# Splitting fifteen of eighty loads into two transfers of unequal partition counts

## The chip, the cores and the metric

The kernel runs on one core of a Trainium2 chip. The metric is the device time of one execution in microseconds, the median over runs. Inputs and outputs are float32; inside, the kernel works largely in bfloat16.

## The reference

A gated linear attention with a recurrent state is followed by a gated MLP that mixes over the sequence. Batch 4, 8 heads, 768 steps, head size 48; the MLP has a width of 384 and 1024 hidden columns.

```python
def _attn_ref(q, k, v, alpha):                    # each (4, 8, 768, 48)
    for t in range(S):
        state = alpha[:, :, t, :, None] * state + einsum('bhd,bhe->bhde', k[:, :, t], v[:, :, t])
        y[:, :, t] = einsum('bhd,bhde->bhe', q[:, :, t], state)

def _moe_ref(x, w_in, w_spatial, b_spatial, w_out):   # x = y as (4, 768, 384)
    h = maximum(x @ w_in, 0)
    u, v = h[..., :512], h[..., 512:]
    v_n = (v - mean(v)) / sqrt(var(v) + 1e-6)
    v_s = einsum('ts,bsd->btd', w_spatial, v_n) + b_spatial[None, :, None]
    return (u * v_s) @ w_out
```

## The kernel before

The sequence is cut into chunks of 128 steps, six to a batch, 24 in all, numbered through (chunk 16 is the fifth of the third batch). For each chunk the kernel loads alpha, k, q and v (tiles `ac`, `kc`, `qc`, `vc`), takes the logarithm of alpha on ACT (`la`, L651), sums it along the chunk on PE, forms exponentials on ACT, scales k on POOL or DVE (`kt`, L681) and q on DVE (`qt`, L691), casts v (`vb`), transposes k and q on PE (L710), multiplies, masks on DVE (`ptm`), and adds the part of the carried state, which POOL and DVE keep (`state`, `sbd`). The first eight chunks go in pairs: one load brings 256 steps (L432, 384 KB), partition p holding steps 2p and 2p + 1 (`pair`, tiles `binvp`, `vbp`). From chunk 8 on each load brings 128 steps (L637, 192 KB): 128 partitions with 8 rows of 192 bytes, one row for each head.

The MLP then follows for each batch: `second_v`, `second_u`, `second_s` (the mixing, with `w_spT` and `vn`) and `second_o`; all its matmuls share L819. Outputs are stored by L1037 and, for the last tile, L1011. Weights come by L1084 in pieces of 768 KB.

What sets the order of the work: every piece of work is an `Op` with a key, and the string `PLAN` lists them in one global order with the engine for each. `replay` emits them in that order, so each engine's instruction stream is fixed by hand. A load is two words of the plan: `S..` for its issue on SP's queue and `Q..` for the transfer. SP works its queue strictly in order, and it waits there for the buffer that a load is to fill (`io_pool`, three buffers of each of `ac`, `kc`, `qc`, `vc`, each for two chunks). All loads and stores but one small one go through SP's queue.

The framework gives each transfer of SP's queue one of eight semaphores in turn, and an issue waits until the eighth transfer before it has landed. An instruction that reads a loaded tile waits for that transfer's semaphore.

Of the kernel before, what the change touches and what calls it, by code (L numbers as in the profile page):

```python
# [50 lines left out]
    "o": {"ACT": 0.4, "DVE": 0.47},  # L51
}
PAIRS = (0, 1, 2, 3)
ACT_STATS = ((2, 2), (1, 4))
LETTERS = {"P": "PE", "D": "DVE", "A": "ACT", "G": "POOL", "S": "SP", "Q": "DMA"}

# [68 lines left out]
def kernel(  # L125
# [12 lines left out]
    nc = tc.nc  # L138

    B, H, S, D = q.shape  # L140
    C = 128
# [143 lines left out]
    def op(key, *args, **kw):  # L285

        users = kw.pop("use", ())
        o = Op(key, *args, **kw)
        for s in users:
            s.users.append(o)  # L290
        ops.append(o)
        made[key] = o
        return o

    def got(*keys):
        return [made.get(x) for x in keys]
# [50 lines left out]
    def finish_x(i):  # L347
# [11 lines left out]

        if i // 2 in PAIRS:  # L360
            def xt(_):
                xv = st["xv"] = st["y"].rearrange("p h d -> p (h d)").bitcast(BF16)[:, 0:KS * 128].rearrange(
                    "p (ks t) -> p ks t", ks=KS)
                for ks in range(KS):
                    nc.tensor.transpose(xv[:, ks, :], st["x_sb"][:, ks, :], ident)  # L365
# [27 lines left out]
        for r in range(2):  # L393
            def xe(eng, r=r):
# [5 lines left out]
                ("xe", i, r), {"ACT": 0.25, "DVE": 0.22}, None, xe,  # L400
                got(("xt", i)) + [made.get(("all", b - 3))], prio=P + 9, use=[sls[r]]))

    def io_users(x, j, back=None):

        j = j - IO if back is None else j
        if x == "cum":
            return got(("cum", 2 * j), ("cum", 2 * j + 1), ("cump", j, 0), ("cump", j, 1), ("updq", j))
        return got((x, 2 * j), (x, 2 * j + 1), (x + "p", j), (x + "p", j, 0), (x + "p", j, 1))
# [5 lines left out]
    def pair(j):  # L414
# [3 lines left out]
        b, c0 = divmod(2 * j, NCH)  # L418
        t0 = c0 * C
# [8 lines left out]
        def load(name, src):  # L428
            def emit(_):
                t = st[name] = io_pool.tile([128, 2, H, D], FP32, name=name).rearrange(  # L430
                    "p a h d -> p (a h d)").rearrange("p (h a d) -> p h a d", h=H, a=2)
                nc.sync.dma_start(  # L432
                    out=t.rearrange("p h a d -> p h (a d)"),
                    in_=src[b, :, t0:t0 + 2 * C, :].rearrange("h (p a) d -> p h (a d)", a=2))
            return emit

        for n, (x, src, u) in enumerate((("ac", alpha, "ln"), ("kc", k, "kt"), ("qc", q, "qt"), ("vc", v, "vb"))):
            dma((x, 2 * j), LP, load(x, src), io_users(u, j), P + 0.1 * n, issue=1.48)
            made[(x, 2 * j + 1)] = made[(x, 2 * j)]
            made[(x, 2 * j + 1, "issue")] = made[(x, 2 * j, "issue")]  # L440

        def ln(_):
            nc.scalar.activation(
                out=lap[:, :, :, 0:D], in_=st["ac"].rearrange("p h two d -> p two h d"), func=AF.Ln)

        op(("lnp", j), "ACT", 0.73, ln, got(("ac", 2 * j), ("c_la", j % NKP)) + io_users("cum", jo, 0), prio=P + 1)
        sl_c = [Slot(ring), Slot(ring)]
        for par in range(2):
# [160 lines left out]
        for ci in range(2):  # L609
            i = 2 * j + ci  # L610
# [14 lines left out]
    def first(i):  # L625
        b, c = divmod(i, NCH)
        t0 = c * C
# [4 lines left out]
        def load(name, src):  # L632
            def emit(_):
                if name + "2" not in st:
                    T[i - i % 2][name + "2"] = T[i + 1 - i % 2][name + "2"] = io_pool.tile([128, 2, H, D], FP32, name=name)
                t = st[name] = st[name + "2"][:, i % 2]
                nc.sync.dma_start(out=t, in_=src[b, :, t0:t0 + C, :].rearrange("h s d -> s h d"))  # L637
            return emit

        j = i // 2  # L640
        jo = j - NKP
        dma(("ac", i), LD, load("ac", alpha), io_users("ln", j), P)
        dma(("kc", i), LD, load("kc", k), io_users("kt", j), P + 0.1)
        dma(("qc", i), LD, load("qc", q), io_users("qt", j), P + 0.2)
# [213 lines left out]
    def second_v(b, tt):  # L858
# [3 lines left out]
        t0 = tt - tt % 2  # L862
        on_act = (b, t0) in ACT_STATS

# [191 lines left out]
    op(("c_id",), "POOL", 0.5, lambda _: make_identity(nc, ident), prio=-19.0)  # L1056
    op(("c_m4",), "POOL", 0.95, c_m4, prio=-8.0 if PAIRS else -18.0)
    op(("c_sbd",), "DVE", 0.62, c_sbd, prio=-9.5)
    op(("c_row",), "DVE", 0.22, c_row, prio=-9.4)
    if PAIRS:  # L1060
        op(("c_half",), "DVE", 0.45, c_half, prio=-18.5)
# [45 lines left out]
    for b in range(B):  # L1107
        for c in range(NCH):
            i = b * NCH + c
            if i // 2 in PAIRS:  # L1110
                if i % 2 == 0:
# [48 lines left out]
```

## Time and profile before

| | |
|---|---|
| time, median of 3 runs | 141.3 us (141.24 to 141.33) |
| span of the profiled execution | 144.3 us; the page gives no other time for it |
| busy: PE, DVE, ACT, POOL | 136.8, 118.7, 106.8, 86.8 us |
| moved by DMA | 28.64 MB in 89000 packets, of which 83728 under 512 B |
| loads of chunks (alpha, k, q, v) | 16 of 384 KB, 64 of 192 KB |
| issue to landing, 192 KB loads | 2.9 us at least, 4.0 in the median, 6.3 at most |

The row of DMA shares in slices is the mean over 16 DMA engines, in tenths. "Issue to landing" runs from the start of the issue on SP to the last of the transfer's semaphore updates. In the list of DMA queues, q1 carries the kernel's own transfers, and those named "instruction" bring the engines' programs. [...]

### The profile page before, as it was taken

What the parts mean: (1) busy time and instruction counts of PE and PEld (TensorE: products, weight loads), DVE (VectorE), ACT (ScalarE), POOL (GpSimd) and SP (SyncE); (2) the same over time, 40 slices, a digit from 0 to 9 for tenths busy, and PEclk for the clock granted to TensorE, in tenths of its full rate; (3) what the DMA queues carried; (4) which work ended last, traced back from release to release, by engine and by line L of the source; (5) the groups of instructions that cost most, each with busy time, mean ns of one, the idle gap of its engine ahead of it and who ended that gap; (6) DMA issues with size and microseconds to landing.
All of it is one profiled execution on the core that took longest, in us unless ns stands there. A gap on an engine that the chain in (4) does not pass through costs nothing.

```text
span 144.3 us, 4963 instructions
## 1 busy us (share of the span) xinstructions
PE 136.8 (95%) x1915; PEld 84.2 (58%) x1915; DVE 118.7 (82%) x289; ACT 106.8 (74%) x278; POOL 86.8 (60%) x152
## 2 busy tenths in 40 slices
PE   7799999799799999999999999999999999999990
PEld 3334766656465765676556665665657666555560
DVE  7015798899999969899999999999979897987940
ACT  3473479899895879899997789998797698861031
POOL 6856179892709979981249789511599687002820
PEclk9999999999999999999999999999999999999998
DMA  4999999929899989999899899799999241090055
GB/s 108 321 326 351 282 250 325 344 58 259 181 269 191 300 164 182 205 181 214 169 211 222 175 174 185 152 204 196 212 239 227 66 172 55 0 354 28 5 191 191
DMA packets 89000, 28.64 MB, mean 198 GB/s; under 512 B 83728, under 2 KB 87440, under 8 KB 88976
## 3 DMA queue, kind: packets, MB, share of 16 engines
q1 hardware_dynamic: 88944, 28.32, 79.5%
q8 instruction: 15, 0.25, 0.7%
q14 instruction: 9, 0.07, 0.1%
q0 software_dynamic: 32, 0.00, 0.0%
HBM read 23.60 MB, written 4.72 MB: 196 GB/s over the span
## 4 chain that ended last, share of the span: by engine, by line
PE 78%; DVE 8%; ACT 5%; DMA 3%; issue 3%; SPq 0%; ACTq 0%; DVEq 0%
PE bank L819 47%; PE bank L188 4%; DMA ac<-in_alpha_dram 3%; PE bank L710 3%; PE bank L452 2%; PE bank L502 2%; PE bank L745 2%; PE bank L574 2%; DVE ptm L756 2%; PE bank L773 2%; PE bank L731 2%; PE bank L544 1%; DVE ptm L585 1%; PE bank L657 1%; PE bank L601 1%
## 5 line engine op out<-in xcount | busy, mean ns | idle before, releaser
L819 PE MATMUL bank<-w_spT,vn 128*128 128x384 bf16 x192 | 36.3, 326 | 0.1
L980 POOL TENSOR_TENSOR gT<-vsb,uT 128x384 bf16<-128x384 f32 x28 | 25.7, 927 | 11.7 <-DVE vsb L967 11.2
L335 POOL TENSOR_TENSOR state<-state,bc 128x192 f32<-128x192 f32 x20 | 10.3, 513 | 21.4 <-DVE state L328 6.2
L819 PEld LDWEIGHTS <-vn 128*128 128x128 bf16 x192 | 17.1, 97 | 10.2 <-issue 0.2
L756 DVE TENSOR_TENSOR ptm<-bank,mask 128x512 bf16<-128x512 f32 x32 | 20.8, 682 | 1.0 <-ACT xT L198 1.0
L819 PE MATMUL bank<-xT,w_in 128*128 128x384 bf16 x96 | 19.4, 326 | 0.0
L967 DVE TENSOR_TENSOR vsb<-bank,bsp_bc 128x384 f32<-128x384 f32 x31 | 16.7, 554 | 3.2 <-PE bank L819 2.8
L819 PE MATMUL bank<-w_in,xT 128*128 128x512 bf16 x72 | 18.8, 379 | 0.0
L198 ACT COPY kqT<-bank 128x512 bf16<-128x512 bf16 x24 | 13.6, 590 | 6.9 <-PE bank L502 4.4
L819 PE MATMUL bank<-w_out_sb,gT 128*128 128x384 bf16 (+1 forms) x100 | 18.4, 320 | 0.1
L681 POOL TENSOR_TENSOR kt<-kc,binv 128x384 bf16<-128x384 f32 x13 | 12.0, 927 | 6.6 <-ACT bc L676 2.7
L200 POOL CAST sbd<-state 64x192 bf16<-64x192 f32 x40 | 13.6, 341 | 2.1
L884 DVE BATCH_NORM_STATS2 stats<-v_sb 128x6 f32<-128x512 bf16 x20 | 13.6, 681 | 0.5 <-ACT v_sb L204 0.5
L204 ACT ACTIVATE v_sb<-bank 128x512 bf16<-128x512 f32 x20 | 11.9, 608 | 1.6 <-PE bank L819 1.6
L198 ACT CAST x_sb<-bank 128x384 bf16<-128x384 f32 x21 | 10.2, 493 | 3.5 <-PE bank L773 2.7
L819 PEld LDWEIGHTS <-w_in 128*128 128x128 bf16 x96 | 8.7, 97 | 6.0
L188 PE MATMUL bank<-junk 128*128 128x512 f32 (+2 forms) x16 | 11.1, 838 | 1.1 <-DVE halves_of L264 1.1
L200 DVE COPY kqT<-bank 128x512 bf16<-128x512 bf16 x24 | 9.2, 415 | 3.1 <-PE bank L502 2.3
L819 PEld LDWEIGHTS <-gT 128*128 128x128 bf16 x100 | 8.7, 97 | 5.1 <-POOL gT L980 0.2
L204 ACT ACTIVATE uT<-bank 128x384 bf16<-128x384 f32 x23 | 11.3, 495 | 0.3 <-PE bank L819 0.2
L198 ACT COPY xT<-bank 128x192 bf16<-128x192 bf16 (+1 forms) x27 | 9.1, 378 | 2.4 <-PE bank L365 1.5
L585 DVE TENSOR_TENSOR ptm<-bank,mask 128x512 bf16<-128x512 f32 x16 | 10.2, 682 | 0.7 <-PE bank L574 0.4
(128 smaller groups left out, 285.2 us busy)
## 6 DMA issues: line engine op xcount, KB each, us to landing
ac<-in_alpha_dram SPq DMA_DIRECT2D x16, 192.0 KB, 3.9
kc<-in_k_dram SPq DMA_DIRECT2D x16, 192.0 KB, 4.2
qc<-in_q_dram SPq DMA_DIRECT2D x16, 192.0 KB, 4.0
vc<-in_v_dram SPq DMA_DIRECT2D x16, 192.0 KB, 3.8
raw_w<-in_moe_w_spatial_dram SPq DMA_DIRECT2D x3, 768.0 KB, 4.5
out_dram<-raw_w SPq DMA_DIRECT2D x11, 192.0 KB, 2.0
out_dram<-o_sb SPq DMA_DIRECT2D x9, 192.0 KB, 1.9
ac<-in_alpha_dram SPq DMA_DIRECT2D x4, 384.0 KB, 5.5
```

The costliest lines, as they stand in the source:

```text
L188: nc.tensor.matmul(out=flat[:, 0:cols].rearrange("p (a b) -> p a b", a=4), lhsT=junk, rhs=junk[:, None, 0:n].to_broadcast([128, 4, n]), st ...
L198: nc.scalar.copy(out=out, in_=in_)
L200: ENG[eng].tensor_copy(out=out, in_=in_)
L204: nc.scalar.activation(out=out, in_=in_, func=AF.Relu)
L335: ENG[eng].tensor_tensor(out=st["state"], in0=st["state"], in1=st["bc"][:, :, None].to_broadcast([128, HP, D]), op=ALU.mult)
L585: nc.vector.tensor_tensor(out=st[f"ptm{par}"][:, s], in0=st[f"pt{s}{par}"], in1=mask2[:, par], op=ALU.mult)
L681: ENG[eng].tensor_mul(out=k_blocks(kt3)[:, :, :, 0:D], in0=quad(st["kc"]), in1=st["binv"])
L756: nc.vector.tensor_tensor(out=st["ptm"][:, s], in0=st[f"pt{s}"], in1=mask4, op=ALU.mult)
L819: return lambda ps: nc.tensor.matmul(out=out(ps), lhsT=lhsT(), rhs=rhs(), start=start, stop=stop)
L884: nc.vector.bn_stats(out=stats, in_=d["v_sb"][:, tt, :])
L967: nc.vector.tensor_tensor(out=hold["vs"], in0=ps[:, 0:TH], in1=bsp_bc[:, th, :], op=ALU.add)
L980: ENG[eng].tensor_tensor(out=bt[b]["gT"][:, dsl, cols], in0=hold["vs"], in1=bt[b]["uT"][:, dsl, cols], op=ALU.mult)
```

## The change

A table `ROWS` names fifteen of the 80 loads, by tile and chunk. Each of them is asked for as two transfers, the first for the partitions below the number in the table and the second for the rest; the two follow one another on SP's queue. All other loads go out as before, through the same new helper `request`. The plan is the same, word for word.

```diff
+ROWS = {("qc", 4): 120, ("ac", 6): 120, ("vc", 6): 120, ("ac", 8): 120, ("ac", 9): 120, ("vc", 11): 104, ("qc", 12): 88,
+        ("kc", 12): 120, ("qc", 13): 126, ("kc", 15): 72, ("qc", 16): 117, ("qc", 18): 121, ("ac", 19): 120,
+        ("kc", 20): 117, ("kc", 18): 88}
...
+    def request(name, i, to, src):
+
+        cut = ROWS.get((name, i), 0)
+        for rows in ((slice(0, cut), slice(cut, 128)) if cut else (slice(0, 128),)):
+            nc.sync.dma_start(out=to[rows], in_=src[rows])
...
-                nc.sync.dma_start(
-                    out=t.rearrange("p h a d -> p h (a d)"),
-                    in_=src[b, :, t0:t0 + 2 * C, :].rearrange("h (p a) d -> p h (a d)", a=2))
+                request(
+                    name, 2 * j, t.rearrange("p h a d -> p h (a d)"),
+                    src[b, :, t0:t0 + 2 * C, :].rearrange("h (p a) d -> p h (a d)", a=2))
...
-                nc.sync.dma_start(out=t, in_=src[b, :, t0:t0 + C, :].rearrange("h s d -> s h d"))
+                request(name, i, t, src[b, :, t0:t0 + C, :].rearrange("h s d -> s h d"))
```

The tiles, the buffers and the bytes moved stay as they are. SP's queue has 126 transfers in place of 111, and an instruction that reads a split load first waits for two semaphores.

## The prediction

> **What bounds the kernel now.** I read the page first (busy time, DMA row, chain), then the chain in order of time, then the waits, then the transfers.
>
> ```profile
> span 144.3 us, 4963 instructions
> PE 136.8 (95%) x1915; PEld 84.2 (58%) x1915; DVE 118.7 (82%) x289; ACT 106.8 (74%) x278; POOL 86.8 (60%) x152
> DMA  4999999929899989999899899799999241090055
> PE 78%; DVE 8%; ACT 5%; DMA 3%; issue 3%; SPq 0%; ACTq 0%; DVEq 0%
> ...
> q8 instruction: 15, 0.25, 0.7%
> ```
>
> Two things are nearly full at once: PE is busy for 95% of the span, and the DMA engines show 9 in most slices up to about 113 us. Yet the chain gives DMA only 3%. That 3% stands at the start, before any split load. In the middle the chain leaves PE for one stretch, from 61.39 to 73.54 us, and there it runs through DVE and ACT:
>
> ```profile
> 1.23 4.23 DMA ac<-in_alpha_dram
> ...
> 61.39 0.35 DVE kqT L200
> ...
> 72.95 0.55 DVE qt L691
> 73.54 2.60 PE bank L819 x15
> ```
>
> The waits say the same. These are the only rows of the list of waits that end on a transfer:
>
> ```profile
> POOL w_row L200 <- DMA raw_w<-in_moe_w_spatial_dram: 2.8, 1, 2.8
> ACT la L443 <- DMA ac<-in_alpha_dram: 2.6, 2, 2.2
> POOL vbp L200 <- DMA vc<-in_v_dram: 1.2, 2, 0.8
> ```
>
> None of those ends on a split load but one of the two of vbp, on POOL (0.40 us, its row is below). So in the traced execution the loads come in time, and the change can gain nothing on the chain as it was traced. The page gives no time for the traced execution beside its span of 144.3 us; the timed runs have a median of 141.3, 3.0 us (2.1%) less. I apply all terms to 141.3. A compute side that runs 2.1% quicker leaves the loads less room than the trace shows, unless they quicken too.
>
> **How much room the loads have.** In the full stretch from 50.1 to 89.7 us SP issues one load after another:
>
> ```profile
> q1 hardware_dynamic: 38985, 7.37, 95.8%
> q8 instruction: 5, 0.08, 0.9%
> ...
> ac<-in_alpha_dram SPq DMA_DIRECT2D x11, 192.0 KB, 3.9
> kc<-in_k_dram SPq DMA_DIRECT2D x10, 192.0 KB, 4.1
> vc<-in_v_dram SPq DMA_DIRECT2D x10, 192.0 KB, 3.8
> qc<-in_q_dram SPq DMA_DIRECT2D x9, 192.0 KB, 4.2
> ```
>
> 40 loads in 39.6 us: one each 0.99 us, so the DMA engines set the pace. With 128 partitions in even shares, 8 for each of 16 engines, one partition costs an engine at most 0.99 / 8 = 0.12 us. The transfers of instructions (q8) are few but large: 0.7% of 16 engines over 144.3 us, through 15, is 144.3 x 16 x 0.007 / 15 = 1.08 us of one engine each. A load is done when its slowest engine is done, so a load that runs beside such a fetch should land about 1.1 us late. The landings, from windows on the issues, show it. First the window 70 to 76 us, which has no q8 packet, then 77.4 to 79 us, whose loads are under way when the one q8 packet of 80 to 81.1 us (third block) is moved:
>
> ```profile
> vc<-in_v_dram SPq DMA_DIRECT2D x4, 192.0 KB, 3.7
> ac<-in_alpha_dram SPq DMA_DIRECT2D x3, 192.0 KB, 3.6
> ...
> qc<-in_q_dram SPq DMA_DIRECT2D x2, 192.0 KB, 5.0
> ...
> q8 instruction: 1, 0.02, 5.5%
> ```
>
> 3.6 to 3.7 us for seven of the first window's eight loads, 5.0 beside a fetch: 1.3 us. The two late loads are those of q for chunks 16 and 18, which the change splits.
>
> **The change, part by part.**
>
> *Fifteen more issues on SP.* A load's issue has these lengths (minimum, median, maximum in ns):
>
> ```profile
> L637 SPq DMA_DIRECT2D kc<-in_k_dram x16: 378/774/1516, 32.7 to 104.5; - x16
> L1037 SPq DMA_DIRECT2D out_dram<-o_sb x9: 332/333/442, 116.3 to 140.6; - x9
> L691 DVEq EVENT_SEMAPHORE  x16: 21/21/50, 44.0 to 115.3; - x16
> L681 POOLq EVENT_SEMAPHORE  x13: 17/17/2582, 44.0 to 112.7; - x13
> ```
>
> The shortest issues are 0.33 to 0.38 us; longer ones are SP being held back while the engines catch up. Two issues, 0.38 + 0.35 = 0.73 us, still fit into the 0.99 us pace: cost 0 in the full stretch. Without that cover it is 0.35 us an issue, 5.3 us in all on SP, of which a load sees only its own and those just ahead. Queued behind on SP are later loads, and from about 95 us the stores; no load after chunk 20's is split, so nothing of it reaches the stores at the end. A second wait on SP is older: each issue waits for the eighth transfer before it. With about four loads under way (3.9 / 0.99), three of them split make seven, so this does not bind.
>
> *Consumers wait for two transfers.* The programs of the two kernels have the same instructions in the same order on PE, DVE, ACT and POOL; net 14 more semaphore waits stand on them (4 on ACT, 5 on DVE, 5 on POOL). By the two rows above that is 14 x 0.02 = 0.3 us over three engines, between 0 and 0.3 on the path; I take 0.1, since of DVE's only the two of chunk 12 lie in the stretch where DVE carries the chain.
>
> *Where the pieces run.* Both pieces move the same bytes. No row shows a transfer of 120 or 88 partitions, so this is bounded from both sides. One end: the pieces use all 16 engines evenly, nothing is relieved, gain 0. The other end: a piece is dealt in equal shares to as many engines as divide its partitions (120 to 15, 126 to 14, 117 and 104 to 13, 72 to 12, 121 and 88 to 11), always the same lowest ones. Then all fifteen loads leave the last engine alone. If the fetches sit on it, their 1.08 us are hidden; in exchange the low engines get more: 120/8 puts 8 + 1 partitions on the first, 0.12 us more than now, and 88/40 or 121/7 puts 12, 0.48 us more. Net relief of a landing beside a fetch: 1.08 - 0.12 = 0.96 us for the mild splits, and for chunk 16's and 18's q together (10 and 12 partitions, six more than now, 0.7 us) 1.08 - 0.7 = 0.4 us. I take the second end as the likelier, because every load in the trace has 128 partitions, whose shares are equal and whole, and for these pieces equal whole shares need a divisor. That the fetches sit on the last engine and not on a low one no row shows; I give it better than half, as a choice.
> The Trainium skill, page "DMA: Bandwidth & Descriptors", section "Why a DMA increments its semaphore by 16 and not by 1", states this rule of the largest divisor up to 16, on the lowest-numbered engines; no row of this trace has such a shape, so the trace neither agrees nor disagrees. Its section "Latency and other measured facts" says that engines 7 and 15 are usually slower than the others; no row here tells the engines apart.
>
> *Who gets the relief.* Take k of chunk 16, the load just behind those two of q:
>
> ```profile
> 82.29 0.67 SPq L637 DMA_DIRECT2D kc<-in_k_dram  x1
> kc<-in_k_dram SPq DMA_DIRECT2D x1, 192.0 KB, 3.7
> 86.19 1.06 POOL L681 TENSOR_TENSOR kt<-kc,binv 128x384 bf16<-128x384 f32 x1 [0.31 <-ACT binv L669]
> 88.07 0.29 PE L710 MATMUL bank<-ident,kt 64*128 64x64 bf16 x8
> 37.46 0.91 POOL L200 CAST vbp<-vc 128x384 bf16<-128x384 f32 x1 [0.40 <-DMA vc<-in_v_dram]
> ```
>
> It lands at 82.29 + 3.7 = 86.0, and POOL uses it at 86.19: 0.2 us of room. The full stretch begins near 39 us; 47 us of compute that is 2.1% quicker gains 1.0 us on loads whose pace is fixed, so in a timed run POOL may wait 0.8 us here. Its result is read by PE at 88.07, 0.8 us after POOL ends at 87.25, so between 0 and 0.8 us reaches PE. A gain at the end thus lies between 0 (as traced) and 0.96 us (one whole relief at one place, since later places have then moved too). I take the middle, 0.5 us: 141.3 - 0.5 + 0.1 = 140.9. The last row is v of chunk 6: its second piece is issued 0.35 us later, no fetch of q8 runs beside it, so POOL's 0.40 us may become 0.75; POOL is not on the chain there: 0.
>
> **Rivals.**
> First, the loads stay hidden in timed runs as in the trace: only the waits count, 141.3 + 0.1 = 141.4. For it: the list of waits. Against it: the 3.0 us between span and time.
>
> Second, slower: the fetches sit on one of the low engines, which the splits load more. Place: k of chunk 16 again. The six extra partitions of the two q loads ahead come on top of the fetch, 0.7 us; POOL then waits 0.8 + 0.7 = 1.5 us, PE's cover takes 0.8, and 0.7 remains: 141.3 + 0.7 + 0.1 = 142.1, and 141.8 if the compute side is only half as much ahead. It decides from the point where that load lands over 1 us later than its use. For it: a mean DMA share of 95.8% leaves the low engines little to spare. Against: between fetches landings are back at 3.6 to 3.7 us, so an engine that is 0.7 us behind catches up within a few loads.
>
> Third, the change does not do what it says: the pieces use all engines, or follow one another on the same ones. No relief, 0.1 us of waits, and 0.35 us of issue where SP is not held back: 141.4 to 141.7.
> The Trainium skill, page "DMA: Bandwidth & Descriptors", section "Rules for kernel authors", speaks against the change: two transfers to disjoint partition halves serialize, and one of 128 partitions is to be used. By that it would be this third rival; no row here has split transfers to test it.
>
> **How the numbers follow.** About 0.2% (0.28 us) can be told from no change, so no change is 141.0 to 141.6. Forecast 0.46, first rival 0.24, second 0.18, third 0.12. Faster takes the forecast and a little of the first rival, in case its waits cost nothing and v of chunk 6 helps: 0.48. Within the bound: most of the first and half of the third: 0.26. Slower: the second, the rest of the third and of the first: 0.26. The range goes from the whole relief, 141.3 - 0.96 = 140.3, to just under the second rival's full price, 142.0. The forecast's own range is 140.3 to 141.0.
>
> **What would show it.** Right: landings of split loads beside a q8 packet near 4.0 us instead of 5.0 (q of chunks 16 and 18), a shorter time for the loads from 50 to 90 us, the same chain, no new DMA waits on POOL or DVE. Wrong: the landing of k of chunk 16 at 4.4 us or more and a wait of POOL L681 or DVE L691 on a DMA (second rival); landings unchanged (third); landings shorter and the time the same (first). A stall on SP in front of an issue that waits for the eighth transfer before it would show the lanes binding, which I excluded.

## The result and the profile after

The change makes the kernel slower: the ratio of the times after to before is 1.008, with a 95% interval of 1.006 to 1.010, so about +1.1 us where I had forecast -0.4. Two runs after the change took 142.42 and 142.50 us, four runs of the kernel before 141.24 to 141.33. Some executions of any of these kernels run 2 to 6 us longer in a disturbed state, and the execution that I read for the prediction (span 144.3 us) was one of them; all ratios here leave these out, and the kernel before is shown below from a second, undisturbed trace, with a span of 139.6 us and a time of 141.36.

The page of the kernel after (time 142.5 us, so 1.8 us lie around the span, as they do around the 139.6 before):

```profile
span 140.7 us, 4991 instructions
PE 133.1 (95%) x1915; PEld 83.0 (59%) x1915; DVE 117.5 (84%) x289; ACT 106.8 (76%) x278; POOL 87.0 (62%) x152
DMA  4999999989989989969899796999988060180055
DMA packets 89096, 28.64 MB, mean 204 GB/s; under 512 B 83824, under 2 KB 87536, under 8 KB 89072
q8 instruction: 15, 0.25, 0.8%
PE 83%; DVE 6%; DMA 3%; POOL 2%; issue 2%; ACT 1%; SPq 0%; ACTq 0%; POOLq 0%
```

The picture is the old one: PE at 95%, the DMA engines nearly full to the middle of the span, 3% of DMA on the chain. Nothing on this page says that loads have become late. The waits of the engines do (engine, line, what it waited for; total, times, longest):

```profile
POOL vbp L203 <- DMA vc<-in_v_dram: 2.2, 3, 0.9
ACT vbp L201 <- DMA vc<-in_v_dram: 0.8, 1, 0.8
DVE qt L490 <- DMA qc<-in_q_dram: 0.7, 1, 0.7
```

In the trace of the kernel before used here, POOL has one such wait of 0.5 us, at 14.8 us for chunk 2, and none for chunk 4; ACT and DVE have none on these lines. The chain in order of time, between 18 and 25 us of the kernel after, shows where it matters (start, length, what):

```profile
19.61 1.78 POOL kt L483 x2
21.39 0.89 issue
...
22.30 0.51 POOL vbp L203
22.80 0.48 POOL state L338
23.28 0.02 issue
23.30 0.36 DVE state L333
```

The chain goes over POOL, stands still for 0.89 us, and goes on with the cast of v of chunk 4 when that load lands. The timelines of the two kernels side by side, the kernel before first:

```profile
19.86 0.55 DVE L481 TENSOR_TENSOR qt<-qc,bank 128x384 bf16<-128x384 f32 x1
21.37 0.50 POOL L200 CAST vbp<-vc 128x384 bf16<-128x384 f32 x1
21.41 0.54 ACT L198 CAST vbp<-vc 128x384 bf16<-128x384 f32 x1
22.38 0.36 DVE L330 TENSOR_TENSOR state<-bank,state 128x192 f32<-128x192 f32 x1
```

and after:

```profile
20.50 0.56 DVE L490 TENSOR_TENSOR qt<-qc,bank 128x384 bf16<-128x384 f32 x1 [0.68 <-DMA qc<-in_q_dram]
22.30 0.51 POOL L203 CAST vbp<-vc 128x384 bf16<-128x384 f32 x1 [0.91 <-DMA vc<-in_v_dram]
22.26 0.51 ACT L201 CAST vbp<-vc 128x384 bf16<-128x384 f32 x1 [0.76 <-DMA vc<-in_v_dram]
23.30 0.36 DVE L333 TENSOR_TENSOR state<-bank,state 128x192 f32<-128x192 f32 x1 [0.70 <-POOL state L338]
```

From here on the recurrent state, and with it everything, is 0.9 us late, and at the end it is 1.1 us (140.7 against 139.6). So in this execution nearly the whole loss is made at 22 us, at the third pair of chunks, and not in the stretch from 50 to 90 us where I had looked.

What stands beside this late load is seen on SP's queue, kernel before first, then after (start and length of the issues; x2 is a split load):

```profile
13.63 1.15 SPq L432 DMA_DIRECT2D qc<-in_q_dram  x1
14.82 1.15 SPq L432 DMA_DIRECT2D vc<-in_v_dram  x1
16.08 2.01 SPq L432 DMA_DIRECT2D ac<-in_alpha_dram  x1
```

```profile
13.58 2.15 SPq L410 DMA_DIRECT2D qc<-in_q_dram  x2
15.78 0.40 SPq L410 DMA_DIRECT2D vc<-in_v_dram  x1
16.29 2.44 SPq L410 DMA_DIRECT2D ac<-in_alpha_dram  x2
```

v of chunk 4 stands between two split loads, q of chunk 4 (120/8) ahead of it and alpha of chunk 6 (120/8) behind it. The second piece of q holds SP for 0.88 us, nearly as long as the whole load did (1.15), although it carries a sixteenth of the bytes, so the issue of v begins 0.96 us later. That issue then takes 0.40 us in place of 1.15 and so ends only 0.2 us later; no run tells which of the two counts. And the DMA engines move less just then. The stretch from 17 to 19 us, before and then after; behind the busy times of the engines come PE's clock, the DMA share (packet time as a share of 16 engines' time, over 1 where packets overlap) and GB/s:

```profile
17.00:19.00 2.00, 2.00 (x67) 1.61 (x67) 1.93 (x4) 1.21 (x4) 1.83 (x5) 1.00 1.09 298
```

```profile
17.00:19.00 2.00, 2.00 (x69) 1.59 (x63) 1.93 (x4) 1.21 (x4) 1.83 (x5) 1.00 1.24 239
```

A fifth fewer bytes in these two microseconds, at more packet time; in the next two it is 247 GB/s against 232 before. In the trace's semaphore updates v of chunk 4 lands at 20.61 us before and at 22.24 after; it is wanted at 21.37. Sixteen updates tell of this load. Fifteen of them are in by 19.60 us before and by 20.66 after; the last one follows 1.01 us behind them before and 1.58 us behind them after.

### The profile page after: what moved, and what is told of

Read it like the earlier page. It is cut to its first block, busy times and chain, and to the rows that moved or that the text cites. A ratio compares the mean times of both kernels' runs of the same rounds, so it can differ in the third digit from the quotient of the medians.

```text
span 140.7 us, 4991 instructions
## 1 busy us (share of the span) xinstructions
PE 133.1 (95%) x1915; PEld 83.0 (59%) x1915; DVE 117.5 (84%) x289; ACT 106.8 (76%) x278; POOL 87.0 (62%) x152
## 2 busy tenths in 40 slices
DMA packets 89096, 28.64 MB, mean 204 GB/s; under 512 B 83824, under 2 KB 87536, under 8 KB 89072
## 4 chain that ended last, share of the span: by engine, by line
PE 83%; DVE 6%; DMA 3%; POOL 2%; issue 2%; ACT 1%; SPq 0%; ACTq 0%; POOLq 0%
PE bank L828 53%; PE bank L191 3%; PE bank L719 3%; PE bank L754 3%; DMA ac<-in_alpha_dram 3%; PE bank L511 2%; PE bank L782 2%; PE bank L740 2%; PE bank L666 2%; PE bank L461 2%; PE bank L392 2%; PE bank L776 2%; PE bank L583 1%; DVE ptm L594 1%; POOL kt L483 1%
## 5 line engine op out<-in xcount | busy, mean ns | idle before, releaser
L338 POOL TENSOR_TENSOR state<-state,bc 128x192 f32<-128x192 f32 x20 | 10.3, 515 | 15.8 <-DVE state L331 6.2
L678 ACT ACTIVATE binv<-bank 128x384 bf16<-128x384 f32 x16 | 7.9, 492 | 2.6 <-PE bank L669 1.8
```

The lines of the kernel that those rows point to most:

```text
L338: ENG[eng].tensor_tensor(out=st["state"], in0=st["state"], in1=st["bc"][:, :, None].to_broadcast([128, HP, D]), op=ALU.mult)
L678: nc.scalar.activation(out=st["binv"], in_=st["cv"], func=AF.Exp, scale=-1.0)
```

## Experiments

Each kernel is the one named with only the table of splits changed, unless its diff says otherwise. Ratios are to the kernel before, timed beside it on the same chip; brackets are 95% intervals.

**The same kernel again, and single early splits.** First a copy of the kernel before, then q of chunk 4 alone, all splits but that one, and the twelve splits of chunks 8 and later.

> The kernel before, unchanged, for a trace that belongs to the timed 141.3 us (a span near 139.5 us, as timed runs stand 1.8 us above their span). All theories: time ratio 1.00. Theory A (the split of q of chunk 4 delays v of chunk 4, the load behind it): here v of chunk 4 lands near 21.0 us and POOL's cast of it, which the changed kernel starts at 22.30 us after a wait of 0.91 us, starts near 21.4 us with no wait. Theory B (the splits from chunk 11 on overload the engine that also moves PE's instructions): chunk 4's cast waits here as well, and the difference opens after 55 us. Theory C (added issues and waits everywhere): the difference grows evenly.

Measured: 1.0003 [0.999, 1.002]. This is the yardstick, and its trace is the "before" above.

```diff
+ROWS = {("qc", 4): 120}                                       # e2, and again as e9
+ROWS = {... all fifteen without ("qc", 4)}                    # e3
+ROWS = {... the twelve of chunks 8 to 20}                     # e4
```

> Only q of chunk 4 is split (120 and 8 partitions). Theory A: all or nearly all of the loss is here, 142.2 to 142.5 us, v of chunk 4 lands over 0.9 us later than without the split, and POOL waits for it. Theory B: 141.3 us. Theory C: one fifteenth of the loss, 141.4 us.

> All splits but that of q of chunk 4. Theory A: no loss, 141.1 to 141.4 us; if the relief of the prediction is real it shows here as 140.9. Theory B: the full loss, 142.4 us. Theory C: fourteen fifteenths of it, 142.4 us.

> Only the twelve splits of chunks 8 and later; the three of 384 KB loads (chunks 4 and 6) are whole. Theory A: 141.1 to 141.4 us; equal to the run without q of chunk 4 if the other two large splits cost nothing, lower if they do. Theory B: 142.4 us. Theory C: twelve fifteenths of the loss, 142.2 us.

Measured: 1.0007 [0.999, 1.002] for q of chunk 4 alone, 1.005 [1.003, 1.007] for all but it, 1.003 [1.001, 1.005] for the late twelve. Theory A in its first form, that q of chunk 4 makes the whole loss, falls: alone it costs little, and without it half the loss remains. Theory B falls as the main cause: the late twelve cost 0.3%, and in their trace PE is within 0.1 us of the kernel before from the start to the end.

**The three early splits, and what kind of split it takes.**

```diff
+ROWS = {("qc", 4): 120, ("ac", 6): 120, ("vc", 6): 120}       # e5
+ROWS = {... the same fifteen loads, each cut at 112}          # e6
+ROWS = {... the table of the change}                          # e7
+ROWS = {... the same fifteen loads, each cut at 115}          # e8
```

> Only the three splits of 384 KB loads are left (q of chunk 4, alpha and v of chunk 6, all 120/8); the other twelve loads go out whole. Theory A2 (the loss is made between 14 and 42 us, where the compute waits for the loads: v of chunk 4 behind the split q, the spatial weight and v of chunk 6 behind the split alpha): nearly the whole loss of the change, +0.8 to +1.2 us on the kernel before. Theory B (the twelve late splits overload the engine of the instruction fetch): +0.1 us or less. Theory C (issues and waits, evenly over the splits): a fifth, +0.2 us.

> The same fifteen loads in two transfers each, at the same places, but cut at 112: both 112 and 16 are multiples of 16, so by the rule of the largest divisor both pieces use all 16 engines evenly, and the packets are 15 x 16 = 240 more than in the kernel before. Theory D (the loss comes from the uneven shares of the engines): back at the kernel before, within 0.3 us. Theory C (the loss comes from the second issue, the second wait and the second set of packets): the same loss as the change, +0.9 to +1.3 us, and v of chunk 4 and the spatial weight land as late as there.

> The changed kernel again, as the yardstick for its neighbours on the same chip: +1.0 to +1.3 us by all theories. In the trace, if the places of the loss are the same in another execution, POOL waits again 0.9 us for v of chunk 4 and over 3 us for the spatial weight.

> The same fifteen loads cut at 115: by the rule of the largest divisor 115 goes to 5 engines (23 partitions each) and 13 to 13 engines, so the lowest five engines carry 24 partitions of a split load in place of 8, and a split load lands at least 1.9 us later (16 x 0.12 us). Theory D (uneven shares): the loss grows to several us, +3 to +8, and the waits on the split loads fill the list of waits. Theory C (issues and waits alone): the same as the change, +1.0 to +1.3 us.

Measured: 1.009 [1.006, 1.012] for the three, 1.010 [1.006, 1.014] for even shares, 1.009 [1.005, 1.013] for the change again, and 1.100 [1.095, 1.104] for the heavier shares. Three things follow. The three early splits alone cost as much as all fifteen (A2). The uneven shares are not needed for the loss: cut into 112 and 16, where both pieces use all 16 engines, the loads cost as much, and v of chunk 4 is late in the same way. That makes 0.7 us of the 1.6 us by which this traced execution is late at the end; the rest arises at 64 and 82 us and is taken up below. The timeline of e6:

```profile
22.05 0.50 POOL L201 CAST vbp<-vc 128x384 bf16<-128x384 f32 x1 [0.60 <-DMA vc<-in_v_dram]
```

Yet the shares are real. The packets of the four pages differ as equal shares over the largest divisor up to 16 would have it, one packet more for each engine of a piece: 89096 for the change (+96 on 89000), and

```profile
DMA packets 89240, 28.64 MB, mean 203 GB/s; under 512 B 83968, under 2 KB 87680, under 8 KB 89216
DMA packets 89030, 28.64 MB, mean 183 GB/s; under 512 B 83758, under 2 KB 87470, under 8 KB 89006
```

for e6 (15 x 16 = 240 more) and e8 (15 x (5 + 13 - 16) = 30 more). For the change the sum is 7 x 7 + 9 + 2 x 5 + 0 + 10 + 2 x 8 + 2 = 96. And where a piece of 115 partitions goes to five engines, 23 to each, the shares do decide, 14 us of them: in the traced execution of e8, of 158.0 us, the chain has DMA at 14% and SP's queue at 12%.

```profile
PE 57%; DMA 14%; SPq 12%; DVE 4%; ACT 4%; issue 4%; POOL 3%; ACTq 0%; POOLq 0%; DVEq 0%
```

The Trainium skill, page "DMA: Bandwidth & Descriptors", section "Why a DMA increments its semaphore by 16 and not by 1", has this rule of the largest divisor; the three packet counts agree with it to the packet. They do not tell which engines these are.

**Which of the three, and through what.** One kernel has q of chunk 4 alone, one the other two, and two move v of chunk 6 ahead of the weight piece that it had to queue behind.

```diff
+ROWS = {("qc", 4): 120}                                       # e9
+ROWS = {("ac", 6): 120, ("vc", 6): 120}                       # e10
-... S33 Q34 G334 P170 A220 S328 Q329 D350 ...                 # e11 (before), e12 (after)
+... S382 Q383 S328 Q329 G145 ...                              # v of chunk 6 behind alpha of chunk 8
```

> Only q of chunk 4 is split (120/8). Theory E (a second piece holds up SP's queue and the transfers behind it, whatever its size; v of chunk 4 is the first load that then comes too late): in an undisturbed trace v of chunk 4 lands near 22 us in place of 20.6, POOL waits 0.7 to 0.9 us for it, POOL's later casts of the weights and so the issue of the second piece of the spatial weight come 0.7 us later; the time +0.4 to +0.8 us. Theory F (chunk 4 costs nothing by itself; the loss needs the split alpha and v of chunk 6): within 0.3 us of the kernel before.

> Only alpha and v of chunk 6 are split (120/8). Theory E: v of chunk 6 lands 0.5 to 1 us later behind the spatial weight, POOL waits for it at about 35 us; +0.4 to +0.8 us. Theory F: nearly the whole loss, +0.9 to +1.2 us.

> The kernel before with one load moved: v of chunk 6 is asked for right behind alpha of chunk 8 (at about 26 us) and no longer behind the second piece of the spatial weight (at about 29 us), where SP waits for a buffer; nothing is split. If the wait of POOL for v of chunk 6 in the kernel before (0.4 us and less) is on nobody's path: within 0.3 us. If the loads of 26 to 36 us set the pace of the compute behind them: 0.3 to 0.8 us quicker, since k and q of chunk 8 land earlier too.

> The changed kernel with the same load moved, so that the split v of chunk 6 has landed long before it is used. Theory E: the part of the loss that comes through v of chunk 6 goes, the part through v of chunk 4 stays: +0.4 to +0.8 us on the kernel before in place of +1.1. If v of chunk 6 has no part in the loss: +1.0 to +1.3 us as before. If the fifteen second issues cost evenly: +1.0 to +1.3 us.

Measured: e9 1.003 [1.000, 1.005], e10 1.002 [1.000, 1.004], e12 1.008 [1.004, 1.011]. e11 gave two times, 141.32 and 141.54, as the kernel before, and no interval. So v of chunk 6 has no visible part in the loss of the change: asked for earlier it brings nothing, neither before nor after. In e10 it lands late as expected, but its wait comes to nothing:

```profile
21.36 0.50 POOL L201 CAST vbp<-vc 128x384 bf16<-128x384 f32 x1
...
35.34 0.51 POOL L201 CAST vbp<-vc 128x384 bf16<-128x384 f32 x1 [0.71 <-DMA vc<-in_v_dram]
```

The second row is chunk 6, 0.72 us later than before (34.62); five microseconds on, POOL is back within 0.05 us. It is not so in every execution. In e3, where q of chunk 4 is whole, ACT waits 0.63 us for v of chunk 6, all that follows is 0.5 us late, and the chain goes through this load:

```profile
29.58 6.95 DMA vc<-in_v_dram
...
36.61 0.51 ACT vbp L199
```

Neither q of chunk 4 nor alpha of chunk 6 by itself makes POOL wait for chunk 4 (the first row, as before; in e9 it starts at 21.43, without a wait). The semaphore updates say why: v of chunk 4 lands at 20.4 to 20.7 us with neither split, at 21.23 (e9), 21.29 (e10) and 21.31 (e3) with one of them, at 22.0 to 22.2 with both (e5, e6, the change). Its use is at 21.4. One split costs it about 0.65 us and both 1.4 to 1.6; its room was 0.76, so one is hidden, and of two 0.6 to 0.9 us come through. The traced executions of e2, e7 and e13 to e15 took 143.7 to 146.3 us; POOL comes to this cast at 23.1 us or later there, after the load has landed, so they do not show the wait, e7 not either, of which it was expected.

How the two do it is seen in part. With q of chunk 4 split (e9), fifteen of the sixteen updates of v are in by 20.44 us in place of 19.60, and the last follows 0.79 us behind. With alpha of chunk 6 split (e3, e10), the fifteen are in by 19.8 to 20.2 us, and the last follows 1.1 to 1.5 us behind. So the one makes the whole load later, and the other mostly its last update. That one update is late already in the kernel before goes along with a transfer of instructions: in eleven traces (e1, e3 to e6, e9 to e12, e16, the change) a packet of 16 KB on q8 starts between 16.3 and 16.9 us, and the last update comes 0.8 to 1.7 us behind the fifteenth; in e17 the packet starts at 15.8 us, and the last update comes 0.1 us behind. That the packet is the reason is likely, but no run moves it, and no row tells the engines apart.

**Both neighbours, and all but one.** This was the test of that account, with a rival that needs v of chunk 6 and one that spreads the loss. The first two kernels were run twice.

```diff
+ROWS = {("qc", 4): 120, ("ac", 6): 120}                       # e13, e16
+ROWS = {... all fifteen without ("ac", 6)}                    # e14, e17
+ROWS = {... all fifteen without ("qc", 4) and ("ac", 6)}      # e15
```

> Only q of chunk 4 and alpha of chunk 6 are split. Theory G (these two lie directly ahead of and behind v of chunk 4 on the queue; each makes it land 0.65 us later; its room in the kernel before is 0.76 us, so one is hidden and two come through): v of chunk 4 lands near 22.1 us, POOL and ACT wait 0.6 to 0.9 us for it, +0.6 to +1.0 us. Theory H (the loss needs v of chunk 6 as well): +0.2 to +0.4 us.

> Only q of chunk 4 and alpha of chunk 6 are split, once more. Theory G: v of chunk 4 lands near 22.1 us and +0.6 to +1.1 us. Theory H (the loss needs v of chunk 6 as well): +0.2 to +0.4 us.

> The change without the split of alpha of chunk 6: fourteen loads are split. Theory G: v of chunk 4 lands near 21.25 us, just before its use; the loss falls from +1.1 to +0.3 to +0.6 us. Theory I (the loss is spread over the splits): +1.0 us.

> The change without the split of alpha of chunk 6, once more. Theory G: v of chunk 4 lands near 21.25 us, with at most 0.2 us of waiting on POOL and ACT; +0.3 to +0.6 us. Theory I (the loss is spread over the splits): +1.0 us.

> The change without the splits of q of chunk 4 and alpha of chunk 6: thirteen loads are split. Theory G: v of chunk 4 lands near 20.6 us as in the kernel before, and +0.4 us at most remain. Theory I: +0.9 us.

Measured: the two alone 1.008 [1.005, 1.011] (e16; e13 had one time, 142.74 us, and no interval). All but alpha of chunk 6: 1.003 [1.000, 1.006] and 1.003 [1.000, 1.006]. The other thirteen: 1.004 [1.000, 1.008]. The timelines of e16 and e17 at the cast of chunk 4:

```profile
22.54 0.50 POOL L201 CAST vbp<-vc 128x384 bf16<-128x384 f32 x1 [1.08 <-DMA vc<-in_v_dram]
```

```profile
21.63 0.50 POOL L201 CAST vbp<-vc 128x384 bf16<-128x384 f32 x1
```

With two splits of fifteen the loss is there. With alpha of chunk 6 taken out of the fifteen two thirds of it are gone, and POOL does not wait for this load; with q of chunk 4 taken out (e3, 1.005) somewhat under half is gone, and what is left in its trace came through v of chunk 6. v of chunk 4 lands at 22.49 us in e16 and 21.34 in e17, in e17 with a share of luck: it is asked for 0.9 us later than in e9, and its last update comes in time. Theory G stands for the place and the two neighbours; H and I fall, though e15 alone would not exclude I. Nor is the whole loss of every trace made at this load: of the 1.9 us by which e16 is late at the end, 1.3 are there by 26 us, and 0.55 arise at 35 us in two casts (see the last section), as 0.5 us do in e5.

The late splits have places too, but not in every execution. Their 0.3% comes from e4 and e15 with intervals that begin at 0.1 and 0.0%; the times of e4 reach from 141.55 to 142.60 us, and in the execution of e4 that was traced the last store goes out 0.05 us later than before, so that trace shows none. In e17 and e6 the chain goes through two loads that are whole and stand behind split ones, alpha of chunk 15 (behind q and k of chunk 12) and q of chunk 17 (behind q of chunks 16 and 18). The first as e17 shows it, then the second as e6 shows it:

```profile
61.06 3.22 DMA ac<-in_alpha_dram
64.31 0.52 ACT la L658
```

```profile
78.95 3.42 DMA qc<-in_q_dram
82.46 0.48 DVE qt L698
```

Each of the two places makes both traces 0.4 to 0.6 us later. In the trace of the kernel before there is no room there either: the two loads land at 63.35 and 80.69 us, 0.02 and 0.09 us before their use. In the trace of the change, which is 1.0 us late by then, the two places cost nothing more. That would be why the early and the late splits, 0.9% and 0.3% alone, make no more than 0.8 to 0.9% together; no run tests it. Also open is why a piece of 24 KB holds SP for about 1 us (0.88 to 1.11 us in the traces of the change, e5, e9, e16 and e17, but 0.40 in e12).

## Why the prediction was wrong, step by step

**"So in the traced execution the loads come in time."** True of that trace, and no forecast. There v of chunk 4 lands at 21.00 us, and POOL casts it at 24.50:

```profile
24.50 0.50 POOL L200 CAST vbp<-vc 128x384 bf16<-128x384 f32 x1
```

That is 3.5 us of room. In the trace of 139.6 us it is 21.37 - 20.61 = 0.76 us. I took the list of waits of one long execution for the answer, and never worked out the room of the split loads and their neighbours themselves; I did it for one load, k of chunk 16, chosen because it lay behind the two loads beside a fetch, and for none in the start. This is the step that failed: my sum has no term for a second piece that makes a load of the start late, and the traces show 0.6 to 0.9 us in its place (the change, e5, e6; 1.1 in e16).

**The 3.0 us between span and time**, from which I made a compute side 2.1% quicker all along, belong to that one execution. Timed runs have a span of 139.6 us and 1.8 us around it, so the execution was 4.7 us too long. Against the trace of 139.6 us its compute is 3.1 us late by 14 us, 4.8 by 36 us, and no later after that: from 40 us on the two go at one pace, and the 1.0 us that I let compute gain between 39 and 86 us is 0. That loads in the middle are nearly late was right, by the places at 64 and 82 us, but my reason for it was not.

**"Cost 0 in the full stretch"** for the second issues held in e4 and in the trace of the change, and did not in e17 and e6. At 14 us it did not hold: loads of 384 KB are issued there one each 1.2 us, the second piece of q took 0.88 to 1.11 us (0.40 in e12) in place of my 0.35, and the transfer rate fell by a fifth for 2 us (298 to 239 GB/s). My 0.35 came from the shortest issues, stores at the end above all. "Queued behind on SP are later loads" was written, and which one comes next was not followed up.

**"Consumers wait for two transfers", 0.1 us:** nothing speaks against it. In e4, with twelve split loads, PE is within 0.1 us all the way.

**"Where the pieces run":** the second end, equal shares on as many engines as divide, was right in the number of engines, as 96 packets more show. Against "the fetches sit on the last engine" speaks that of the pieces of q of chunk 16, on 13 and 11 engines, one engine in each reports 0.70 us after all others beside the fetch of 75.5 us (from their semaphore updates; no row shows single engines). If the pieces lie on the lowest engines, as I assumed, the fetch lies on one of the eleven lowest, and the splits leave it its work. q of chunk 16 lands 4.4 us after its first issue in place of 3.9, and v of chunk 4, the load that cost the time, has its last update 1.58 us behind the others in place of 1.01. The relief that my forecast lived on, 0.5 us of the sum, shows in no run.

**k of chunk 16,** the place of my gain and of the second rival's loss, saw neither in the trace of the change. Its use on POOL, before and after:

```profile
82.58 0.91 POOL L681 TENSOR_TENSOR kt<-kc,binv 128x384 bf16<-128x384 f32 x1 [1.50 <-ACT vb L198]
```

```profile
83.65 0.91 POOL L690 TENSOR_TENSOR kt<-kc,binv 128x384 bf16<-128x384 f32 x1 [1.58 <-DMA kc<-in_k_dram]
```

It is 1.07 us later, and 1.0 of that was there by 26 us. In both traces it starts 0.16 us after its load has landed (82.42 and 83.49 us), so its room is as small as I had said. The second rival had the sign right, and its price (142.1) came near by chance, since that time was lost at another place. In e6 and e17 its neighbourhood did cost 0.4 and 0.5 us, at q of chunk 17 just ahead; e6 has even shares, so the extra partitions on low engines that this rival rests on are not needed for it.

**v of chunk 6,** "0.40 us may become 0.75; POOL is not on the chain there: 0", was right in size and in effect in e10 (0.71 us, and nothing of it left at the end), and not in e3, where the chain goes through this load.

**The third rival** (no relief, waits and issues only, up to 141.7) came nearest in kind: a second transfer that brings nothing and costs its issue. The Trainium skill, page "DMA: Bandwidth & Descriptors", section "Rules for kernel authors", advises one transfer of 128 partitions in place of two to disjoint halves; e6 agrees, where two pieces on all 16 engines cost 1.0%. I gave it 12%, and priced the issue at the idle queue's 0.35 us.

## What to carry to other kernels

For each transfer that an edit touches, for the one ahead of it and for the next two behind it on the same queue, subtract the landing from the first use; a list of waits shows only where that room is already gone. Delays that are hidden one by one come through when two fall on the same load: 0.1 to 0.3% each and 0.8% together here, so half of an edit that "costs nothing" proves little about the whole. Room that is read in one execution is the room of that execution: 3.5 and 0.76 us for the same load of the same kernel here. A span that stands apart from the timed median is a reason to trace again, not a term of the sum.

## What the runs showed of the hardware that I had not expected

While loads follow one another, a small second piece holds SP nearly as long as a whole load: 2.15 to 2.4 us for the two issues of q of chunk 4 in place of 1.15, with 24 KB as with 48 KB (e12 is the exception, with 1.7).

The order in which DVE and POOL begin two casts can be worth 0.5 us. When the second piece of the spatial weight lands, both cast rows of it from float32. If DVE starts first (32.97 against 33.03 us before), POOL's cast takes 1.64 us and DVE's two take 1.02:

```profile
33.03 1.64 POOL L200 CAST w_row<-raw_w 128x768 bf16<-128x768 f32 x1 [2.75 <-DMA raw_w<-in_moe_w_spatial_dram]
32.97 1.02 DVE L200 CAST w_row<-raw_w 128x768 bf16<-128x768 f32 x2
```

If POOL starts first, as in e9, POOL's takes 0.82 and DVE's two 1.49:

```profile
32.99 0.82 POOL L201 CAST w_row<-raw_w 128x768 bf16<-128x768 f32 x1 [2.62 <-DMA raw_w<-in_moe_w_spatial_dram]
33.21 1.49 DVE L201 CAST w_row<-raw_w 128x768 bf16<-128x768 f32 x2
```

DVE is on the path here, POOL is not, so in e9, which was 0.24 us late ahead of these casts, all that follows is 0.7 us late. A quarter of a microsecond can so cost twice as much again. The Trainium skill, page "SBUF — State Buffer", section "SBUF: two separate sides", says that the two engines share a pair of ports as a lock, held for a whole instruction by whichever begins first, where DVE runs in one of its two-port modes; the four rows agree, though none shows DVE's mode.
